# Second MLP product as seven half-size products per 512 tokens, streamed over the feature blocks

## The chip, the cores and the metric

The kernel runs on one core of a Trainium2 chip. The metric is the device time of one execution in microseconds (us). Engines are named as the profile names them: PE is TensorE (matmul), PEld its weight load, DVE is VectorE, ACT is ScalarE, POOL is GpSimd, SP is SyncE, which only issues DMAs here. Each engine takes its instructions strictly in the order in which they stand in its queue.

## The reference

An attention over 8 batches, 8 heads, 576 tokens and head size 64 feeds an MLP with 4608 tokens, width 512 and 2048 features:

```python
scores = scale * np.matmul(q, k.transpose(0, 1, 3, 2))
thresh = np.max(scores, axis=-1, keepdims=True) - tau
scores = np.where(scores >= thresh, scores, -1000000000.0)
attn = softmax(scores)                 # exp, sum, 1e-9 in the denominator
x = matmul(attn, v)                    # heads side by side: 4608 x 512
h = x @ w_in                           # first product, 512 x 2048
g = h * np.tanh(softplus(h))           # the gate, called Mish
return (g @ w_out).astype(np.float32)  # second product, 2048 x 512
```

The inputs q, k and v are float32; w_in and w_out are float64 and reach the chip as pairs of 32-bit words.

## The kernel before

Every large product is done with split operands: an operand is a rounded high part plus a low part with the rest, and of the four partial products three are made (high by high, high by low, low by high), accumulated in PSUM. Splitting costs a cast to the high part (on ACT, here and there on DVE) and a subtraction for the low part (on DVE or POOL).

The program has three stretches. For most of the span attention tiles run, and between them the first product of an earlier batch is fed in small portions by a generator (`gemm1`, `advance`). Its result h goes from PSUM to the staging tile `hst` (four feature blocks of 128 x 288) and by DMA to DRAM tiles `hd`, one for each 288 tokens. The last batch's first product is 384 matmuls, issued as 32 units of 12 (the loop over `u`, L780); in that loop the preparation of the second product is placed by tables of unit numbers (`PACE`, `H0`, `GATES`, `H1`, `GATES1`). Then comes the second product (L839 to L855).

Preparing w_out means decoding float64: ACT scales both words (`first`, L134 and L135), DVE clamps, shifts and joins the sign (L138, L141, L148), POOL adds the low word (L151), ACT casts the high part (L154), and DVE or POOL subtracts for the low part (L157). Before, this is done in 32 portions of 128 x 256, ordered by output block `d`: the first output block's weights are decoded in the last batch's loop, the rest during the first part of the second product. Preparing h means a DMA from `hd` (`load_h`), Mish on ACT (L679), a cast (L681 on DVE or L683 on ACT) and a subtraction on DVE (L684).

The second product goes over chunks of tokens, 256, then eight of 512, then 256. For each chunk and each of four output blocks one PSUM bank takes 3 x 16 matmuls; DVE copies it out (L854) and SP stores it. That is 1920 matmuls, 1536 with 512 columns and 384 with 256.

The lines behind which everything stands are few:

```python
for a, b in ((wh, gh), (wh, gl), (wlo, gh)):
    nc.tensor.matmul(o[:, :m], a, b, start=n == 0, stop=n == 3 * NF - 1)
```

SBUF is handed over between the stretches. The pool `wr` lies where the attention's tiles were; `er` opens in the 18th unit, where the first half of the first product's weights was; `wl` opens after the last unit, where `hst`, the split x and the other half of those weights were, so that a tile in it can be written only after the first product's last matmul and its last stores.

Of the kernel before, what the change touches and what calls it, by code (L numbers as in the profile page):

```python
# [5 lines left out]
F32 = mybir.dt.float32  # L6
# [31 lines left out]
NC = 512  # L38
PACE = {(0, 1, 2, 3, 5, 6, 8, 9, 16, 18, 20, 22, 27, 28)[i]: i for i in range(NF // 2 + 6)}
H0 = (2, 4, 11, 18)  # L40
GATES = (10, 17, 21, 24)
H1 = (8, 9, 22, 23)
GATES1 = (13, 15, 19, 20, 27, 29)
GATES2 = (1, 3)
CHUNKS = (0, *range(256, B * S, NC), B * S)
# [114 lines left out]
def attention_moe(tc, q, k, v, tau, w_in, w_out, out):  # L160
# [3 lines left out]
    with ExitStack() as outer:  # L164
# [3 lines left out]
        hd = [dram.tile([P, NF, HB], F32, name=f"hd{i}") for i in range(NBLK)]  # L168
# [6 lines left out]
        with ExitStack() as first:  # L175
# [6 lines left out]
            with ExitStack() as att:  # L182
# [262 lines left out]
                def gemm1(b, xs, pool=psh, tag="ph", first=1):  # L445
# [12 lines left out]
                    def parts(c, f, ds):  # L458
                        if (c, f) not in banks:
                            banks[c, f] = pool.tile([P, 512], F32, name="h", tag=tag)  # L460
# [198 lines left out]
            pso = second.enter_context(tc.tile_pool(name="pso", bufs=6, space=PSUM))  # L659

            def slot(pool, shape, kind, tag="g"):

                return pool.tile(shape, kind, name="g", tag=tag, bufs=2 if tag == "g" else 1)

            def small(kind, shape):
                return wr.tile(shape, kind, name="ht", tag="ht", bufs=2)

            def load_h(ht, c, fs):

                at, end = CHUNKS[c], CHUNKS[c + 1]  # L670
                while at < end:
                    i, off = divmod(at, HB)
                    m = min(HB - off, end - at)
                    to = at - CHUNKS[c]
                    nc.sync.dma_start(ht[:, :, to:to + m], hd[i][:, fs, off:off + m])
                    at += m

            def gate(ht, gh, gl, engine, vector=False):
                nc.scalar.activation(ht, ht, AF.Mish)  # L679
                if vector:  # L680
                    nc.vector.tensor_copy(gh, ht)  # L681
                else:
                    nc.scalar.copy(gh, ht)  # L683
                engine.tensor_tensor(gl, ht, fv(gh), ALU.subtract)  # L684

            def quarter(k):
                return slice(4 * k, 4 * k + 4)

            def weights2(pool, d):
                return [pool.tile([P, NF, P], F32R, name=f"w2{n}{d}") for n in "hl"]  # L690

            n0 = CHUNKS[1]
            w2 = [weights2(wr, 0)]
            homes = []
            for tag in "ab":
                four = slot(wr, [P, 4, 4 * WC], U32, tag)
                homes += [four[:, i] for i in range(4)]
            g0 = [slot(wr, [P, NF, n0], F32R) for _ in "hl"]
            work = {}
            h0 = {}  # L700
            h1 = {}
            g1 = []
            QUARTER = NF // 2

            def fetch(i):

                if i >= ND * QUARTER:
                    return
                if i < QUARTER:
                    st = homes[i]  # L710
                elif (i - QUARTER) % 6 < 4:
                    st = homes[4 + (i - QUARTER) % 6]
                else:
                    st = small(U32, [P, 4 * WC])
                work[i] = Decode(nc, st, None, None)
                d, k = divmod(i, QUARTER)
                for e in range(2):
                    f = 2 * k + e
                    src = w_out[f * P:(f + 1) * P, d * P:(d + 1) * P].bitcast(U32).rearrange("p (n t) -> p n t", t=2)
                    nc.sync.dma_start(work[i].words[:, e * P:(e + 1) * P], src)  # L720

            def middle(i):
                work[i].clamp()
                work[i].shift()
                work[i].sign()
                work[i].add()

            def finish(i, upper, lower):
                d, k = divmod(i, QUARTER)
                hi, lo = (w[:, 2 * k:2 * k + 2].rearrange("p f n -> p (f n)") for w in w2[d])  # L730
                work[i].hi, work[i].lo = hi, lo
                if upper is nc.scalar:
# [6 lines left out]
                elif i >= QUARTER:  # L739
                    fetch(i + 6)  # L740
# [161 lines left out]
```

## Time and profile before

| | |
|---|---|
| runs shown, median (lowest to highest) | 1371.6 us (1370.14 to 1371.99) |
| span of the profiled execution, which is its own time | 1370.5 us |
| PE busy | 1352.6 us (99%) |
| PEld / DVE / ACT / POOL busy | 1225.3 / 1001.6 / 943.0 / 771.8 us |
| first and last matmul of the second product start at | 968.41 and 1366.95 us |
| last batch's first product, 384 matmuls of 288 columns | about 917.4 to 968.4 us |

PE's busy time is summed from matmul records that overlap, since matmuls are pipelined: a 512-column matmul has a record of 392 ns, while about 220 of them start in 50 us. What a matmul costs is therefore read as the distance between starts. In the grouped rows a group's idle time and its releaser say what the engine waited for just before.

### The profile page before, as it was taken

How to read it: one execution, taken by the hardware profiler on the slowest of the kernel's cores; microseconds unless marked ns; L12 is line 12 of the kernel's file. 1: busy time of each engine (PE TensorE's matmuls, PEld its weight loads, DVE VectorE, ACT ScalarE, POOL GpSimd, SP SyncE). 2: the span in 40 equal slices, each digit the busy share in tenths (PEclk: the TensorE clock that was granted, in tenths of full speed). 3: DMA queues.
4: the chain of work that ended last, by engine and by line, in shares of the span. 5: the costliest groups of instructions: out<-in, count | busy, mean ns of one | idle time of the engine just before them, and what ended most of it. 6: DMA issues, size and time to landing. Idle time of an engine off the chain costs nothing.

```text
span 1370.5 us, 27694 instructions
## 1 busy us (share of the span) xinstructions
PE 1352.6 (99%) x8839; PEld 1225.3 (89%) x8839; DVE 1001.6 (73%) x2976; ACT 943.0 (69%) x2106; POOL 771.8 (56%) x1115
## 2 busy tenths in 40 slices
PE   9998899999999999999999999999999999999999
PEld 7555889999999999999999999999887888888888
DVE  6999999999999999999999999957874332232210
ACT  5878788888888888888888888856555543443210
POOL 5778888778788787887887878633460000000000
PEclk9999999999999999999999999999999999999999
DMA  5333323333333233332332323128655553543310
GB/s 152 98 98 107 114 80 114 108 96 103 101 99 115 89 120 93 111 107 97 103 112 88 124 90 110 60 88 277 196 164 151 153 148 102 143 131 102 93 52 23
DMA packets 126017, 154.64 MB, mean 113 GB/s; under 512 B 23472, under 2 KB 109488, under 8 KB 125872
## 3 DMA queue, kind: packets, MB, share of 16 engines
q1 hardware_dynamic: 124720, 148.16, 36.1%
q10 hardware_dynamic: 1152, 4.72, 0.9%
q8 instruction: 70, 1.15, 0.4%
q14 instruction: 75, 0.61, 0.1%
HBM read 105.64 MB, written 47.19 MB: 112 GB/s over the span
## 4 chain that ended last, share of the span: by engine, by line
PE 84%; DVE 5%; ACT 4%; DMA 2%; issue 2%; POOL 2%; SPq 1%; ACTq 0%; DVEq 0%; POOLq 0%
PE h L94 25%; PE o L851 23%; PE s L94 13%; PE y L94 12%; PE tp L94 9%; PE t L94 1%; DVE st L94 1%; DVE g L94 1%; DVE p L94 1%; DVE dec L94 1%; POOL w2l L157 1%; DMA ht<-hd 1%; DMA g<-hd 1%; ACT e L94 1%; DMA g<-w_out 1%
## 5 line engine op out<-in xcount | busy, mean ns | idle before, releaser
L851 PE MATMUL o<-g,w2h 128*128 128x512 f32 (+1 forms) x1280 | 363.9, 370 | 0.8 <-DVE g L684 0.8
L94 PE MATMUL h<-xh,w1h 128*128 128x288 f32 x1024 | 302.8, 296 | 1.1 <-ACT hst L94 0.6
L94 PE MATMUL h<-xh,w1l 128*128 128x288 f32 x1024 | 302.6, 296 | 0.0
L94 PE MATMUL h<-xl,w1h 128*128 128x288 f32 x1024 | 302.6, 295 | 0.0
L94 POOL TENSOR_SCALAR p<-p,st 128x576 f32<-128x576 f32 x288 | 243.8, 846 | 58.2 <-DVE st L94 33.8
L851 PEld LDWEIGHTS o<-g,w2h 128*128 128x128 f32 x1280 | 231.7, 188 | 43.7 <-DVE g L684 1.1
L94 PE MATMUL s<-k,q 128*128 128x288 f32 (+1 forms) x1280 | 255.2, 324 | 8.2 <-DVE p L94 7.9
L94 DVE SCALAR_TENSOR_TENSOR p<-s,st,e 128x576 f32<-128x576 f32 x288 | 235.1, 816 | 20.5 <-ACT e L94 11.0
L94 ACT ACTIVATE e<-s,st 128x576 f32<-128x576 f32 x288 | 214.2, 744 | 36.0 <-DVE st L94 30.4
L851 PE MATMUL o<-g,w2l 128*128 128x512 f32 (+1 forms) x640 | 236.2, 369 | 0.0
L94 DVE TENSOR_REDUCE st<-s 128x1 f32<-128x576 f32 x288 | 216.7, 752 | 2.6 <-PE s L94 2.5
L94 PEld LDWEIGHTS s<-k,q 128*128 128x128 f32 (+1 forms) x1280 | 182.7, 190 | 38.1 <-DVE p L94 23.6
L94 DVE TENSOR_TENSOR lo<-tp,hi 128x512 fp32r<-128x512 f32 (+1 forms) x280 | 174.7, 632 | 49.2 <-ACT hi L94 42.5
L94 PEld LDWEIGHTS h<-xh,w1h 128*128 128x128 f32 x1024 | 193.1, 189 | 1.9 <-ACT hst L94 1.1
L94 PEld LDWEIGHTS h<-xh,w1l 128*128 128x128 f32 x1024 | 193.0, 188 | 0.0
L94 PEld LDWEIGHTS h<-xl,w1h 128*128 128x128 f32 x1024 | 192.9, 188 | 0.0
L94 PE MATMUL tp<-ident,p 128*128 128x128 f32 x1152 | 174.4, 274 | 3.3 <-DVE lo L94 2.1
L94 ACT CAST hi<-tp 128x512 fp32r<-128x512 f32 (+1 forms) x280 | 149.7, 545 | 36.1 <-PE tp L94 33.1
L684 DVE TENSOR_TENSOR g<-ht,g 128x1024 fp32r<-128x1024 f32 (+1 forms) x60 | 68.6, 1153 | 137.0 <-ACT g L683 137.0
L94 PEld LDWEIGHTS tp<-ident,p 128*128 128x128 f32 x1152 | 138.9, 140 | 13.4 <-issue 5.4
L679 ACT ACTIVATE ht<-ht 128x1024 f32<-128x1024 f32 (+1 forms) x60 | 60.2, 1003 | 115.5 <-DMA ht<-hd 111.0
L851 PEld LDWEIGHTS o<-g,w2l 128*128 128x128 f32 x640 | 120.3, 188 | 21.3
(87 smaller groups left out, 2223.0 us busy)
## 6 DMA issues: line engine op xcount, KB each, us to landing
hd<-hst SPq DMA_DIRECT2D x56, 576.0 KB, 3.4
r<-q SPq DMA_DIRECT2D x120, 160.0 KB, 2.3
r<-k SPq DMA_DIRECT2D x120, 160.0 KB, 2.3
ht<-hd SPq DMA_DIRECT2D x52, 288.0 KB, 3.2
r<-v SPq DMA_DIRECT2D x56, 160.0 KB, 2.3
dec<-w_in SPq DMA_DIRECT2D x32, 256.0 KB, 2.8
out_t<-ost SPq DMA_DIRECT2D x32, 256.0 KB, 2.9
g<-w_out SPq DMA_DIRECT2D x48, 128.0 KB, 3.0
```

The source lines that it names most:

```text
L94: made = method(*args, **kwargs)
L157: engine.tensor_tensor(self.lo, fv(self.a), fv(self.hi), ALU.subtract)
L679: nc.scalar.activation(ht, ht, AF.Mish)
L684: engine.tensor_tensor(gl, ht, fv(gh), ALU.subtract)
L851: nc.tensor.matmul(o[:, :m], a, b, start=n == 0, stop=n == 3 * NF - 1)
```

## The change

The second product is cut into halves along tokens (256 + 256), features (8 blocks + 8 blocks) and outputs (256 + 256), and Strassen's scheme in its variant with shared sums forms the four quarter results from seven products of sums in place of eight. For each pair of feature blocks (`j` and `j + 8`) and each 512 tokens one step `n` of the loop takes seven products x two output blocks x three split terms = 42 matmuls of 256 columns. There are 72 steps (9 chunks of tokens times 8 feature pairs). Fourteen accumulators of 128 x 256 fill seven PSUM banks over eight steps; then `leave` adds them into the four quarters on DVE (the first on ACT) and stores them.

The operands are sums. For each weight pair `j`, `split_w` makes four sums of 128 x 256 on DVE, ACT casts all seven operands at once (128 x 1792), and DVE (odd `j`) or POOL (even `j`) subtracts. For each step `n`, `combine` does Mish on 128 x 1024, one subtraction 128 x 512 on DVE and two 128 x 256 on POOL; `split_z` casts 128 x 1792 on ACT and subtracts 128 x 1792 on DVE. The split operands of a step have three homes, one each in `wr`, `er` and `wl`. A scratch of six tiles of 8 KB a partition holds both raw weights and raw h; a load waits for one of them to come free. The DRAM tiles become `[128, 8, 2, 256]`, one for each 256 tokens, so that a step reads 2 KB runs, and a store of 288 tokens is cut into two pieces. In the last batch all `hst` copies are on ACT. The decode is in portions of 128 x 512, and its places are in the table `steps` (units) and `late` (steps).

```diff
-NC = 512
...
-CHUNKS = (0, *range(256, B * S, NC), B * S)
+NJ = NF // 2
+QT = 256
+NG = B * S // (2 * QT) * NJ
+PRODUCTS = ((0, 1), (4, 5), (5, 3), (3, 4), (6, 0), (2, 6), (1, 2))
...
-        hd = [dram.tile([P, NF, HB], F32, name=f"hd{i}") for i in range(NBLK)]
+        hd = [dram.tile([P, NJ, 2, QT], F32, name=f"hd{i}") for i in range(B * S // QT)]
...
+                def store(queue, hst, at, f):
+                    half, j = divmod(f, NJ)
+                    off, end = 0, HB
+                    while off < end:
+                        i, to = divmod(at + off, QT)
+                        m = min(QT - to, end - off)
+                        queue.dma_start(hd[i][:, j:j + 4, half, to:to + m], hst[:, :, off:off + m])
+                        off += m
...
-                        if b < B - 1 or f % 2:
-                            nc.scalar.copy(hst[:, f % 4], h[:, :HB])
-                        else:
-                            nc.vector.tensor_copy(hst[:, f % 4], h[:, :HB])
+                        nc.scalar.copy(hst[:, f % 4], h[:, :HB])
                         if f % 4 == 3:
-                            queue = nc.sync if b < B - 1 else nc.scalar
-                            queue.dma_start(hd[2 * b + c][:, f - 3:f + 1, :], hst)
+                            store(nc.sync if b < B - 1 else nc.scalar, hst, (2 * b + c) * HB, f - 3)
...
+            def bank(name):
+                i = taken[0] % 8
+                taken[0] += 1
+                if i < 6:
+                    return pso.tile([P, 512], F32, name=name, tag=f"o{i}")
+                return shared(name)
+            def scratch(name):
+                return wr.tile([P, 2048], F32, name=name, tag="z", bufs=6)
...
+            def load_w(j):
                 for e in range(2):
+                    y = scratch("w").bitcast(U32)
+                    words = y[:, 1024:].rearrange("p (n t) -> p n t", t=2)
+                    f = j + e * NJ
+                    nc.sync.dma_start(
+                        words, w_out[f * P:(f + 1) * P].bitcast(U32).rearrange("p (n t) -> p n t", t=2)
+                    )
+                    parts[j, e] = (y, words, y[:, 512:1024], y[:, :512])
+            def convert(j):
+                for e in (1, 0):
+                    _, words, a, _ = parts[j, e]
+                    top, low = words[:, :, 1], words[:, :, 0]
+                    nc.scalar.activation(fv(a), fv(top), AF.Copy, scale=2.0**-112)
+                    nc.scalar.activation(low, low, AF.Copy, scale=2.0**-29)
+            def compose(j):
+                for e in (1, 0):
+                    _, _, a, b = parts[j, e]
+                    nc.vector.tensor_scalar(fv(b), fv(a), TOP_MAX, -TOP_MAX, ALU.min, ALU.max)
+                    nc.vector.tensor_scalar(a, b, 3, 0x7FFFFFF8, ALU.logical_shift_left, ALU.bitwise_and)
+                    nc.vector.scalar_tensor_tensor(b, b, 0x80000000, a, ALU.bitwise_and, ALU.bitwise_or)
+                y, wy, ay, by = parts[j, 1]
+                _, wx, ax, bx = parts[j, 0]
+                nc.gpsimd.tensor_tensor(ay, by, wy[:, :, 0], ALU.add)
+                nc.gpsimd.tensor_tensor(ax[:, QT:], bx[:, QT:], wx[:, QT:, 0], ALU.add)
+                nc.gpsimd.tensor_tensor(y[:, QT:2 * QT], bx[:, :QT], wx[:, :QT, 0], ALU.add)
+            def split_w(j, engine):
+                y, a21 = fv(parts.pop((j, 1))[0]), fv(parts.pop((j, 0))[2])[:, QT:]
+                y = y.rearrange("p (n t) -> p n t", t=QT)
+                nc.vector.tensor_tensor(y[:, 4], a21, y[:, 3], ALU.add)
+                nc.vector.tensor_tensor(y[:, 6], a21, y[:, 1], ALU.subtract)
+                nc.vector.tensor_tensor(y[:, 5], y[:, 4], y[:, 1], ALU.subtract)
+                nc.vector.tensor_tensor(y[:, 7], y[:, 2], y[:, 5], ALU.subtract)
+                home = homes["wr" if j < 4 else "er" if j < 5 else "wl"]
+                w2[j] = [home.tile([P, 7, QT], F32R, name=f"w2{n}{j}") for n in "hl"]
+                nc.scalar.copy(w2[j][0], y[:, 1:])
+                engine.tensor_tensor(w2[j][1], y[:, 1:], fv(w2[j][0]), ALU.subtract)
+            def load_z(n):
+                if n < NG:
+                    c, j = divmod(n, NJ)
+                    z[n] = scratch("z").rearrange("p (n t) -> p n t", t=QT)
+                    for at, i in ((0, 2 * c + 1), (2, 2 * c)):
+                        nc.sync.dma_start(z[n][:, at:at + 2], hd[i][:, j])
+            def combine(n):
+                if n < NG:
+                    y = z[n]
+                    nc.scalar.activation(y[:, :4], y[:, :4], AF.Mish)
+                    nc.vector.tensor_tensor(y[:, 4:6], y[:, :1].to_broadcast([P, 2, QT]), y[:, 1:3], ALU.subtract)
+                    nc.gpsimd.tensor_tensor(y[:, 6], y[:, 1], y[:, 5], ALU.subtract)
+                    nc.gpsimd.tensor_tensor(y[:, 7], y[:, 6], y[:, 3], ALU.subtract)
+            def split_z(n):
+                if n < NG:
+                    home = homes[("wr", "er", "wl")[n % 3]]
+                    g[n] = [home.tile([P, 7, QT], F32R, name=f"g{m}", tag=f"g{m}") for m in "hl"]
+                    y = z.pop(n)
+                    nc.scalar.copy(g[n][0], y[:, 1:])
+                    nc.vector.tensor_tensor(g[n][1], y[:, 1:], fv(g[n][0]), ALU.subtract)
+            homes["wr"] = wr
+            steps = {}
+            for j in range(5):
+                steps.setdefault(max(0, 4 * j - 8), []).append(lambda j=j: load_w(j))
+                steps.setdefault(4 * j + 1, []).append(lambda j=j: convert(j))
+                steps.setdefault(4 * j + 3, []).append(lambda j=j: compose(j))
+            for j in range(5):
+                steps.setdefault(4 * j + 6, []).append(lambda j=j: split_w(j, nc.vector if j % 2 else nc.gpsimd))
+            steps.setdefault(13, []).append(lambda: load_w(5))
+            steps.setdefault(17, []).append(lambda: load_w(6))
+            for n in range(2):
+                steps.setdefault(20 + n, []).append(lambda n=n: load_z(n))
+            steps.setdefault(24, []).append(lambda: convert(5))
+            steps.setdefault(25, []).append(lambda: compose(5))
+            steps.setdefault(26, []).append(lambda: combine(0))
+            steps.setdefault(27, []).append(lambda: split_z(0))
+            steps.setdefault(28, []).append(lambda: combine(1))
+            steps.setdefault(29, []).append(lambda: convert(6))
+            steps.setdefault(29, []).append(lambda: split_z(1))
+            steps.setdefault(30, []).append(lambda: compose(6))
...
-            stream = gemm1(B - 1, batches[B - 1], pso, "o", 4)
+            stream = gemm1(B - 1, batches[B - 1], bank, 4)
...
+        late = {
+            0: [lambda: split_w(5, nc.vector), lambda: load_w(7), lambda: load_z(2), lambda: load_z(3), lambda: combine(2)],
+            1: [lambda: split_w(6, nc.gpsimd), lambda: load_z(4)],
+            2: [lambda: convert(7)],
+            3: [lambda: compose(7)],
+            4: [lambda: split_w(7, nc.vector)],
+        }
...
+            if k == 0:
+                sums["c"] = held()
+                nc.scalar.copy(sums["c"], o)
+            elif k == 1:
+                sums["u"] = held()
+                add(sums["u"], o, sums["c"])
+            elif k == 2:
+                sums["v"] = held()
+                add(sums["v"], o, sums["u"])
+            elif k == 3:
+                value = held()
+                add(value, o, sums["v"])
+                put(value, 1, 1)
+                add(sums["u"], o, sums["u"])
+            elif k == 4:
+                add(sums["u"], o, sums["u"])
+                put(sums["u"], 0, 1)
+            elif k == 5:
+                add(sums["v"], sums["v"], o, ALU.subtract)
+                put(sums["v"], 1, 0)
+            else:
+                add(sums["c"], o, sums["c"])
+                put(sums["c"], 0, 0)
+
+        for n in range(NG):
+            c, j = divmod(n, NJ)
+            for step in late.get(n, ()):
+                step()
+            if n > 0:
+                load_z(n + 4)
+            combine(n + 3)
+            split_z(n + 2)
+            if j == 0:
+                banks = [bank("o").rearrange("p (n t) -> p n t", t=QT) for _ in PRODUCTS]
+            for k, (wi, gi) in enumerate(PRODUCTS):
+                for b in range(2):
+                    at = slice(b * P, (b + 1) * P)
+                    for i, (x, y) in enumerate(((0, 0), (0, 1), (1, 0))):
+                        nc.tensor.matmul(
+                            banks[k][:, b], w2[j][x][:, wi, at], g[n][y][:, gi],
+                            start=j == b == i == 0, stop=j == NJ - 1 and b == 1 and i == 2,
+                        )
+                if j == NJ - 1:
+                    leave(k, c, banks[k])
+            g.pop(n)
```

Three places in the engines' queues matter. The first is ACT in the last batch's loop, where weights are decoded between the copies of h out of PSUM (`hst<-h`) and their stores. Before:

```order
L94 ACTIVATE g<-g 128x256 x2
L94 CAST w2h_15356<-g 128x256
L94 COPY hst<-h 128x288
L94 DMA hd_77<-hst 128x1152
L94 ACTIVATE g<-g 128x256 x2
L94 CAST w2h_15356<-g 128x256
L94 COPY hst<-h 128x288
```

Now (`w` is the scratch of a weight pair, `w2h` its cast):

```order
L90 ACTIVATE w<-w 128x512 x4
L90 COPY hst<-h 128x288
L90 CAST w2h_15623<-w 128x1792
L90 COPY hst<-h 128x288 x2
L90 DMA hd_79<-hst 128x4x32
L90 DMA hd_80<-hst 128x4x256
L90 COPY hst<-h 128x288
```

A pair's whole cast, which needs all the sums of that pair, now stands in one piece ahead of the next copies of h, and each store is two issues.

The second is POOL in the same loop, with the tiles' numbers. Before, three of the rows are low parts of weights (`w2l`), each of 128 x 256, and the others are additions of low words:

```order
L94 TENSOR_TENSOR w2l0_15357<-g_15358,w2h0_15356 128x256
L94 TENSOR_TENSOR g_15358<-g_15358 128x256
L94 TENSOR_TENSOR w2l0_15357<-g_15358,w2h0_15356 128x256
L94 TENSOR_TENSOR g_15359<-g_15359 128x256 x2
L94 TENSOR_TENSOR w2l0_15357<-g_15359,w2h0_15356 128x256
```

Now the first three rows add the low words of pair 0, the fourth is pair 0's low part, and the next three belong to pair 1:

```order
L90 TENSOR_TENSOR w_15416<-w_15416 128x512
L90 TENSOR_TENSOR w_15414<-w_15414 128x256
L90 TENSOR_TENSOR w_15416<-w_15414 128x256
L90 TENSOR_TENSOR w2l0_15540<-w_15416,w2h0_15539 128x1792
L90 TENSOR_TENSOR w_15420<-w_15420 128x512
L90 TENSOR_TENSOR w_15418<-w_15418 128x256
L90 TENSOR_TENSOR w_15420<-w_15418 128x256
```

Pair 1's additions stand behind pair 0's low part, which waits for ACT's cast of pair 0.

The third is ACT where the first product ends and the second begins; `gh_16014` belongs to step 1, `gh_16102` to step 2, `z_16088` and `z_16091` are the raw h of steps 2 and 3, and `hst_16008` is the last staging tile:

```order
L90 CAST gh_16014<-z_15856 128x1792
L90 COPY hst_16008<-h_16018 128x288
L90 COPY hst_16008<-h_16041 128x288
L90 COPY hst_16008<-h_16055 128x288
L90 DMA hd16_79<-hst_16008 128x4x32
L90 DMA hd17_80<-hst_16008 128x4x256
L90 CAST w2h5_16080<-w_15687 128x1792
L90 ACTIVATE z_16088<-z_16088 128x1024
L90 ACTIVATE z_16091<-z_16091 128x1024
L90 CAST gh_16102<-z_16088 128x1792
```

The cast for step 2 stands behind the cast of weight pair 5, which is written into `wl`, and behind the Mish of step 3. Before, the same stretch of this queue held portions of 128 x 256 of the second output block's weights and the Mish and casts of the second chunk.

More of the change, by code (lines that the diff above doesn't have):

```diff
@@ L443, in split_x, with shared, gemm1 @@
                     return parts
-                def gemm1(b, xs, pool=psh, tag="ph", first=1):
+                def shared(name):
+                    return psh.tile([P, 512], F32, name=name, tag="ph")
+                def store(queue, hst, at, f):
[6 more added lines that the diff above has]
+                        off += m
+                def gemm1(b, xs, bank=shared, first=1):
                     halves = (range(NF // 2), range(NF // 2, NF))
@@ L459, in parts @@
                         if (c, f) not in banks:
-                            banks[c, f] = pool.tile([P, 512], F32, name="h", tag=tag)
+                            banks[c, f] = bank("h")
                         h = banks[c, f]
@@ L678, in gate @@
[L678 to L690, printed above, removed]
@@ L774, in attention_moe @@
-            for i in range(QUARTER):
-                fetch(i)
+            pso = second.enter_context(tc.tile_pool(name="pso", bufs=1, space=PSUM))
+            taken = [0]
+            def bank(name):
[6 more added lines that the diff above has]
+                return wr.tile([P, 2048], F32, name=name, tag="z", bufs=6)
@@ L821, in attention_moe @@
-        for i in range(QUARTER, ND * QUARTER):
-            if QUARTER + 6 <= i + 2 < ND * QUARTER:
-                work[i + 2].first()
-            if QUARTER + 6 <= i + 1 < ND * QUARTER:
-                middle(i + 1)
-            if i - QUARTER in GATES2:
-                gate_h1(6 + GATES2.index(i - QUARTER))
-            finish(i, nc.scalar, nc.gpsimd)
-        h2 = slot(wr, [P, 8, NC], F32, "a")
-        for k in range(2):
-            load_h(h2[:, quarter(k)], 2, quarter(k))
-        ready = {0: [[g[:, quarter(q)] for g in g0] for q in range(4)], 1: [(pair[:, 0], pair[:, 1]) for pair in g1]}
@@ L834, in attention_moe @@
-        last = len(CHUNKS) - 2
-        steps = [(c, (d,), range(0)) for d in range(ND) for c in range(2)]
-        steps[-3] = (*steps[-3][:2], range(1))
-        steps[-1] = (*steps[-1][:2], range(1, 4))
-        steps += [(c, range(ND), range(4)) for c in range(2, last + 1)]
-        for c, ds, qs in steps:
-            if c < last:
-                ready.setdefault(c + 1, []).extend(make_g(c + 1, q, h2 if c == 1 and q < 2 else None) for q in qs)
-            m = CHUNKS[c + 1] - CHUNKS[c]
-            g = ready[c]
-            for d in ds:
-                o = pso.tile([P, NC], F32, name="o")
-                n = 0
-                for f in range(NF):
-                    wh, wlo = (w[:, f] for w in w2[d])
-                    gh, gl = (x[:, f % 4] for x in g[f // 4])
-                    for a, b in ((wh, gh), (wh, gl), (wlo, gh)):
-                        nc.tensor.matmul(o[:, :m], a, b, start=n == 0, stop=n == 3 * NF - 1)
-                        n += 1
-                ost = wl.tile([P, NC], F32, name="ost", bufs=2)
-                nc.vector.tensor_copy(ost[:, :m], o[:, :m])
-                nc.sync.dma_start(out[d * P:(d + 1) * P, CHUNKS[c]:CHUNKS[c + 1]], ost[:, :m])
+        wl = homes["wl"] = second.enter_context(tc.tile_pool(name="wl", bufs=1, side="left"))
@@ new lines, in attention_moe, with held @@
+        late = {
[5 more added lines that the diff above has]
+        }
+        places = out.rearrange("(n p) t -> p n t", p=P)
+        def held():
+            return wl.tile([P, 2, QT], F32, name="c", tag="c", bufs=6)
+        sums = {}
@@ new lines, in leave, with put, add @@
+        def leave(k, c, o):
+            def put(value, n, half):
+                at = (2 * c + half) * QT
+                nc.sync.dma_start(places[:, 2 * n:2 * n + 2, at:at + QT], value)
+            def add(to, a, b, op=ALU.add):
+                nc.vector.tensor_tensor(to, a, b, op)
+            if k == 0:
[21 more added lines that the diff above has]
+                put(sums["c"], 0, 0)
```

130 lines of the change are left out of this document (9 added, 121 removed).

## The prediction

> **What bounds the kernel now.** I read the page first, then the chain of waits and the busy times by stage.
>
> ```profile
> span 1370.5 us, 27694 instructions
> PE 1352.6 (99%) x8839; PEld 1225.3 (89%) x8839; DVE 1001.6 (73%) x2976; ACT 943.0 (69%) x2106; POOL 771.8 (56%) x1115
> ...
> 1046.07 321.17 PE o L851 x1493
> ```
>
> PE sets the time, and the chain's last piece is the second product alone, for 321 us without a break. What it costs is read from the stages and from starts in the timeline (start, us, instruction).
>
> ```profile
> 917.40:968.40 51.00, 49.94 (x370) 49.08 (x369) 33.72 (x67) 30.90 (x64) 14.33 (x18) 1.00 0.86 268
> 968.40:1367.10 398.70, 397.94 (x1922) 333.66 (x1920) 138.94 (x173) 152.18 (x196) 35.88 (x44) 1.00 0.41 118
> 1200.00:1250.00 50.00, 50.00 (x220) 41.03 (x219) 13.47 (x14) 18.23 (x18) 0.00 (x0) 1.00 0.39 111
> ...
> 968.41 0.40 PE L851 MATMUL o<-g,w2h 128*128 128x256 f32 x2
> 1344.48 0.40 PE L851 MATMUL o<-g,w2h 128*128 128x256 f32 x2
> 1366.95 0.28 PE L851 MATMUL o<-g,w2l 128*128 128x256 f32 x1
> ```
>
> A 512-column matmul takes 50/220 = 0.227 us of the line. The last chunk's 192 matmuls of 256 columns take 1366.95 - 1344.48 = 22.5 us for 191 intervals, 0.117 us each: half the columns cost slightly more than half, though each loads its own weights. The second product runs from 968.41 to 1367.23 us, 398.8 us; 1536 x 0.227 + 384 x 0.117 = 394 of that is work, so hardly anything is waited for at the seam. In the 51 us ahead of it (first row: PE, PEld, DVE, ACT, POOL busy) DVE, ACT and POOL have room.
>
> **The gain.** The new product is 72 x 42 = 3024 matmuls of 256 columns: 3024 x 0.117 = 353.8 us, 45.0 less than 398.8. Columns fall by an eighth, and part of that goes back because all matmuls are now short. Stretches of this row's kind vary from 0.115 to 0.120, which makes 348 to 363.
>
> **What preparation costs.** Prices for the new sizes come from these rows.
>
> ```profile
> L679 ACT ACTIVATE ht<-ht 128x1024 f32<-128x1024 f32 x52 | 55.1, 1060 | 103.9 <-DMA ht<-hd 99.4 <-DVE ost L854 4.4
> L683 ACT CAST g<-ht 128x1024 fp32r<-128x1024 f32 x52 | 54.0, 1049 | 35.3 <-PE o L851 34.1
> L683 ACT CAST g<-ht 128x512 fp32r<-128x512 f32 x8 | 4.9, 620 | 12.4 <-PE o L851 12.2
> L684 DVE TENSOR_TENSOR g<-ht,g 128x1024 fp32r<-128x1024 f32 x52 | 63.2, 1224 | 124.1 <-ACT g L683 124.1
> L684 DVE TENSOR_TENSOR g<-ht,g 128x512 fp32r<-128x512 f32 x8 | 5.5, 692 | 12.9 <-ACT g L683 12.9
> L94 DVE TENSOR_SCALAR ht<-ht 128x256 uint32<-128x256 uint32 x2 | 0.6, 294 | 0.1
> 945.60 0.69 DVE L94 CAST g<-g 128x1024 fp32r<-128x1024 f32 x1 [1.67 <-DMA ht<-hd]
> L94 POOL TENSOR_TENSOR ht<-ht 128x256 uint32<-128x256 uint32 x2 | 1.5, 744 | 7.8 <-ACT g L135 6.7 <-DVE ht L94 1.1
> L94 POOL TENSOR_TENSOR k<-r,k 128x320 fp32r<-128x320 f32 x120 | 104.6, 877 | 9.9 <-ACT k L94 6.7
> ```
>
> ACT: 0.62 us for 512 elements and, by the slope (1049 - 620)/512, 1.7 for 1792. DVE with two inputs: 0.43 for 256, 0.69 for 512, 2.0 for 1792; with one input 0.43 for 512, between 0.29 for 256 and 0.69 for 1024. POOL: 0.75 for 256, and by (877 - 744)/64 ns an element 1.3 for 512 and 3.8 for 1792.
>
> When DVE and POOL work at once, both slow down:
>
> ```profile
> 978.44 1.85 DVE L681 CAST g<-g 128x1024 fp32r<-128x1024 f32 x2 [1.77 <-DMA hd<-hst]
> 978.77 5.49 POOL L157 TENSOR_TENSOR w2l<-g,w2h 128x256 fp32r<-128x256 f32 x4 [1.23 <-ACT w2h L94]
> 980.21 3.44 DVE L684 TENSOR_TENSOR g<-g 128x1024 fp32r<-128x1024 f32 x2
> ```
>
> Four POOL subtractions take 5.5 us instead of 3.0, two DVE subtractions beside them 3.4 instead of 2.45. Together they get through 0.7 + 0.55 = 1.25 engines' work, not 2.
>
> **One weight pair.** The queues put pair j+1's additions on POOL behind pair j's low part. From the end of DVE's sums of an even pair: ACT cast 1.7, POOL low part 3.8, POOL additions of the next pair 1.3 + 0.75 + 0.75, DVE's four sums 1.4 (the first under the last addition): 9.7. From an odd pair: cast 1.7, DVE low part 2.0, DVE decode of the next pair 2 x (0.43 + 0.43 + 0.69) = 3.1, POOL's last two additions 1.5, sums 1.4: 9.7. Overlap of DVE with POOL adds by the rows above some 0.3 to the first and 1.0 to the second: 20.7 us for two pairs. The table allows four units of 12 x 0.133 = 1.6 us, 6.4 a pair. So the units don't set this pace; the chain does.
>
> ```profile
> 917.60 1.57 POOL L94 TENSOR_TENSOR xl<-x,xh 128x288 fp32r<-128x288 f32 x2 [0.55 <-ACT xh L94]
> 919.20 8.47 SPq L720 DMA_DIRECT2D g<-w_out  x16
> 922.23 0.77 ACT L94 ACTIVATE g<-g 128x256 f32<-128x256 f32 x2 [4.37 <-DMA g<-w_out]
> L94 ACT ACT_TABLE_LOAD x1 | 1.3, 1283 | 0.0
> L94 ACT COPY hst<-h 128x288 f32<-128x288 f32 x240 | 93.9, 400 | 36.8 <-PE h L94 35.7
> hd<-hst ACTq DMA_DIRECT2D x7, 576.0 KB, 4.9
> out_t<-ost SPq DMA_DIRECT2D x32, 256.0 KB, 2.9
> ```
>
> The loads start at 919.2, when POOL leaves the attention's tiles, in both kernels. The first 128 KB were there after 3.0 us. Pair 0 is 1 MB, at the stage's 268 GB/s 3.9 us: about 924. Conversion 0.6, decode 3.1 + 0.4, two additions 1.5 and sums 1.4 give 931 for pair 0's sums, and 931 + 2 x 20.7 = 972.4 for pair 4's.
>
> **Step 0, +19.9 us.** Its raw h needs the scratch tile that pair 4's sums release. Load 3.5 (2.9 plus the second issue): 975.9. ACT meanwhile casts pair 4, converts pair 5, copies h and loads the table: 979.4. Mish 1.06, DVE 0.69 (0.5 late behind pair 5's decode), two POOL subtractions behind pair 5's additions: 984.4; cast 1.7, low part 2.0: 988.3 against 968.41. The first product ends late too, at some 977, because its copies out of PSUM wait on ACT behind the casts; that is hidden under the same wait. Step 1 is ready in time.
>
> **Step 2, +14.0.** Its tile is in `wl`. On ACT the last copies of h stand behind step 1's cast (992.3), so the last store is issued at 994.1 and lands 4.9 later, at 999. Then come the cast of pair 5 (DVE's sums for it end at 1000.7), 1002.5; DVE's low part, 1004.6, which frees the tile for step 3's raw h; that load, 1008.1; step 3's Mish, which stands ahead of step 2's cast, 1009.2; cast 1010.8, low part 1013.3 with overlap. PE finishes step 1 at 999.4.
>
> **Steps 3, 5 and 6, +10.4.** Each step needs 2.75 of ACT and 2.7 of DVE in 4.9, which fits, but pairs 6 and 7 still have 4 to 9 us of casts, decodes, sums and low parts ahead in the queues. Step 3 waits 4.1, step 5 2.0, step 6 4.3.
>
> **The rest, +5.0.** At the end of each chunk DVE has seven more operations from PSUM, 7 x 0.69 = 4.8. Over eight steps that is 8 x 2.7 + 4.8 = 26.4 of 39.3 us, so it hides under PE, with 3.0 at the edges and 0.9 for a bank in step 0. Without this cover (every overlap stretched) DVE's 26.4 and POOL's 8 x 1.5 would fill 38.4 of 39.3. After the last matmul two additions of 0.7 and a store of 2.9 to 3.0 follow, 4.4 instead of 3.3: +1.1. The 16 copies of h that move from DVE to ACT, 0.4 each, are in ACT's 979.4. The doubled stores of h on SP and the smaller runs cost nothing in the long stretch: they wait for the same copies, and two `hst` tiles cover them. If the cover went, ACT would stand there too.
>
> Sum: 1370.5 - 45.0 + 19.9 + 14.0 + 10.4 + 5.0 = 1374.8 us of span. The median shown is 1.1 above the profiled span: **1376 us**.
>
> The TensorE clock is 1.00 in every stage quoted, and no PE wait here is long enough to test it. The Trainium skill, TensorE: Matmul & The Clock Gate, HAM oscillation, says that an idle gap over about 3.4 us drops PE to half clock until it has been busy as long. Three of my gaps are longer; two are followed by another wait that takes the loss up, so by this page the sum would be about 2 us more.
>
> **Rivals.**
>
> Slow overlap is absent. With the bare row prices the pair chain is 18.9 for two, step 0 starts at 983.6 (+15.2), step 2 costs 12.0, the later steps 7.2, the rest 2.9: 1362.8, or 1364 against the runs. For it stands the mean of POOL's additions in the last batch's loop, hardly above 744 ns:
>
> ```profile
> L94 POOL TENSOR_TENSOR g<-g 128x256 uint32<-128x256 uint32 x12 | 9.5, 795 | 34.8 <-DVE g L94 27.0 <-ACT g L94 4.9 <-DMA g<-w_out 1.8
> ```
>
> Against: there POOL is idle most of the time, and the two rows above are from where it is not. Chance 0.22.
>
> The units do set the pace. If the chain kept 6.4 us a pair, all would be ready at 968.4 and only the end and chunk edges remain: 1370.5 - 45.0 + 5.0 = 1330.5, 1332 against the runs. For it: POOL is busy only 14.3 us in the 51 before. Against: it needs 9.7 us of dependent rows to fit 6.4. Chance 0.08.
>
> DVE and POOL exclude each other. If one waits wholly for the other, two pairs take 22.5, step 0 starts at 994.3 (+25.9), step 2 waits 15.3, steps 3 to 7 16, and DVE's 26.4 plus POOL's 12 leave about 1 us per chunk, so the edges cost 13 and the end 1.1: 1397, 1398 against the runs. It decides from where overlap costs more than the whole shorter operation. For it: the four POOL rows. Against: there the four of POOL, the two subtractions and the two casts of DVE, 3.0 + 2.45 + 1.4 = 6.85 us one after the other, were done in 5.8. Chance 0.20. The Trainium skill, SBUF — State Buffer, Who interferes with whom, speaks for it: the port pair that DVE (with two SBUF inputs) and GpSimd share is an exclusive lock, and the later one fully blocks. The rows show it in part.
>
> **How the numbers follow.** The forecast has 0.50, with its own range 1366 to 1386 (0.115 to 0.120 a matmul is -6 to +9, the start of the loads ±2). A run can be told from no change at 0.2%, 2.7 us. Faster: 0.08, most of the 0.22 and a little of the forecast, 0.30. Slower: 0.20 and 0.30 of the forecast, 0.50. Same: 0.20. The range reaches to the two overlap rivals' ends, 1360 to 1398, and leaves out the units' rival and the outer edges.
>
> **What would show it.** Right: PE starts at 0.117 in steady stretches; first L-o matmul near 988 with `gl` on DVE named as releaser; a second wait of some 14 us after two steps; casts of `w2h` waiting for DVE and POOL about 10 us apart. Wrong: a first step before 975, a pair in under 8 us, a pitch of 0.13 or more (0.01 is 30 us), or waits at every chunk.

## The result and the profile after

The changed kernel takes 1386.3 us (1386.04 to 1386.82) against 1371.8 (1370.14 to 1373.15) of the kernel before, run beside it: 1.0106 times as long, 95% interval 1.0092 to 1.0121. It is slower by 1.1%. Its profiled execution spans 1384.1 us, 13.6 more than the one before.

The page of the changed kernel: its span, the busy times, and the strips of PE and of the granted clock, in which a dip stands where the first product meets the second. The last two rows are the costliest groups of the second product, with the idle time ahead of them.

```profile
span 1384.1 us, 30033 instructions
PE 1320.4 (95%) x9943; PEld 1254.4 (91%) x9943; DVE 1139.4 (82%) x3027; ACT 999.3 (72%) x2075; POOL 915.7 (66%) x1227
...
PE   9998899999999999999999999998657999999998
...
PEclk9999999999999999999999999999889999999999
...
L90 PE MATMUL o<-gh,w2h 128*128 128x256 f32 x1008 | 285.8, 284 | 23.3 <-ACT gh L90 21.5
...
L90 PE MATMUL o<-gl,w2h 128*128 128x256 f32 x1008 | 285.7, 283 | 9.6 <-DVE gl L90 9.6
```

The chain of waits ends, as before, with one unbroken piece of PE (start, us):

```profile
1065.74 309.41 PE o L90 x2634
```

That is 0.1175 us a matmul. From 1065.74 on PE is always fed, so the arithmetic that was saved was saved in time too. Nearly everything lost lies before; only the end, from the last matmul to the end of the span, takes 5.4 us instead of 3.3. The busy times by stage of the changed kernel (window, its length, then PE, PEld, DVE, ACT, POOL, granted clock, DMA share, GB/s):

```profile
917.40:968.40 51.00, 44.18 (x310) 43.48 (x310) 36.68 (x45) 25.24 (x46) 20.32 (x16) 0.93 0.58 189
968.40:1000.00 31.60, 18.04 (x113) 17.12 (x113) 17.92 (x23) 15.94 (x24) 13.16 (x12) 0.78 0.42 128
1000.00:1040.00 40.00, 22.16 (x156) 21.05 (x156) 27.88 (x27) 17.12 (x15) 21.34 (x15) 0.83 0.34 105
1080.00:1200.00 120.00, 120.00 (x1024) 120.00 (x1024) 80.83 (x70) 67.02 (x53) 50.63 (x50) 1.00 0.43 135
```

In the timeline of the changed kernel the second product starts at 989.44 and waits for over 1 us at steps 0, 2, 3, 5 and 6 (start, us, instruction, in brackets the idle time before it and who ended it; the rows between are left out):

```profile
989.44 0.58 PE L90 MATMUL o<-gh,w2h 128*128 128x256 f32 x1 [7.90 <-ACT gh L90]
991.50 0.58 PE L90 MATMUL o<-gl,w2h 128*128 128x256 f32 x1 [1.48 <-DVE gl L90]
1014.58 0.58 PE L90 MATMUL o<-gh,w2h 128*128 128x256 f32 x1 [11.36 <-ACT gh L90]
1016.64 0.58 PE L90 MATMUL o<-gl,w2h 128*128 128x256 f32 x1 [1.48 <-DVE gl L90]
1027.03 0.38 PE L90 MATMUL o<-gl,w2h 128*128 128x256 f32 x1 [2.94 <-DVE gl L90]
1039.68 0.39 PE L90 MATMUL o<-gl,w2h 128*128 128x256 f32 x1 [1.82 <-DVE gl L90]
1047.10 0.38 PE L90 MATMUL o<-gh,w2h 128*128 128x256 f32 x1 [2.25 <-ACT gh L90]
1049.16 0.58 PE L90 MATMUL o<-gl,w2h 128*128 128x256 f32 x1 [1.68 <-DVE gl L90]
```

A step has one matmul that needs only the cast (`gh`); then it waits for the low part (`gl`), which comes 2 us later. The start is set by the weight pairs. These rows of the same timeline are ACT's cast of pairs 0, 1 and 4 (two rows left out between), each right behind the pair's sums:

```profile
931.11 1.71 ACT L90 CAST w2h<-w 128x1792 fp32r<-128x1792 f32 x1 [0.32 <-DVE w L90]
942.03 1.69 ACT L90 CAST w2h<-w 128x1792 fp32r<-128x1792 f32 x1 [4.59 <-DVE w L90]
...
974.54 1.69 ACT L90 CAST w2h<-w 128x1792 fp32r<-128x1792 f32 x1 [6.78 <-DVE w L90]
```

Four pairs in 43.4 us, 10.9 each. Why it takes so long shows between the first two, in POOL's low part of pair 0 and DVE's decode of pair 1:

```profile
932.89 4.10 POOL L90 TENSOR_TENSOR w2l<-w,w2h 128x1792 fp32r<-128x1792 f32 x1 [3.29 <-ACT w2h L90]
932.92 4.35 DVE L90 TENSOR_SCALAR w<-w 128x512 uint32<-128x512 uint32 x1
936.94 1.50 POOL L90 TENSOR_TENSOR w<-w 128x512 uint32<-128x512 uint32 x1
937.31 1.69 DVE L90 SCALAR_TENSOR_TENSOR w<-w 128x512 uint32<-128x512 uint32 x1
```

DVE's shift, 0.43 us by itself, has a record of 4.35 us. It ends 0.3 us after POOL's 4.10. The next one, 0.69 by itself, takes 1.69 beside POOL's 1.50. A blocked instruction counts as busy here: DVE's busy time contains its waiting.

### The profile page after: what moved, and what is told of

Read it like the earlier page. It is cut to its first block, busy times and chain, and to the rows that moved or that the text cites. A ratio compares the mean times of both kernels' runs of the same rounds, so it can differ in the third digit from the quotient of the medians.

```text
span 1384.1 us, 30033 instructions
## 1 busy us (share of the span) xinstructions
PE 1320.4 (95%) x9943; PEld 1254.4 (91%) x9943; DVE 1139.4 (82%) x3027; ACT 999.3 (72%) x2075; POOL 915.7 (66%) x1227
## 5 line engine op out<-in xcount | busy, mean ns | idle before, releaser
L90 PE MATMUL o<-gh,w2h 128*128 128x256 f32 x1008 | 285.8, 284 | 23.3 <-ACT gh L90 21.5
L90 PE MATMUL o<-gl,w2h 128*128 128x256 f32 x1008 | 285.7, 283 | 9.6 <-DVE gl L90 9.6
L90 PE MATMUL o<-gh,w2l 128*128 128x256 f32 x1008 | 284.7, 282 | 0.0
L90 POOL TENSOR_TENSOR z<-z 128x256 f32<-128x256 f32 x144 | 148.4, 1036 | 200.1 <-DVE z L90 194.4
L90 DVE SCALAR_TENSOR_TENSOR p<-s,st,e 128x576 f32<-128x576 f32 x288 | 235.1, 816 | 21.3 <-ACT e L90 11.7
L90 DVE TENSOR_TENSOR gl<-z,gh 128x1792 fp32r<-128x1792 f32 x72 | 148.5, 2062 | 110.6 <-ACT gh L90 110.6
L90 ACT CAST gh<-z 128x1792 fp32r<-128x1792 f32 x72 | 121.9, 1693 | 151.4 <-POOL z L90 81.7
L90 PEld LDWEIGHTS o<-gh,w2h 128*128 128x128 f32 x1008 | 193.9, 192 | 24.4 <-ACT gh L90 22.1
L90 PEld LDWEIGHTS o<-gl,w2h 128*128 128x128 f32 x1008 | 193.8, 192 | 11.2 <-DVE gl L90 11.2
L90 PEld LDWEIGHTS o<-gh,w2l 128*128 128x128 f32 x1008 | 193.9, 192 | 0.0
```

The costliest lines, as they stand in the source:

```text
L90: made = method(*args, **kwargs)
```

## The experiments

Theory A: DVE and POOL hardly ever work at the same time on these operations, so the preparation at the seam is one amount of work for the two together, and an operation on POOL costs its own, longer time. Theory B: it is a chain of dependent instructions, which only has to be put in another order. Further rivals were that POOL's help pays (C), that the second product itself loses time, and that half clock after idle time does (H).

**Low parts later.** The low part of pairs 0 to 4 moves behind the next pair's decode.

```diff
-                engine.tensor_tensor(w2[j][1], y[:, 1:], fv(w2[j][0]), ALU.subtract)
+                lows[j] = lambda: engine.tensor_tensor(w2[j][1], y[:, 1:], fv(w2[j][0]), ALU.subtract)
...
+            for j in range(5):
+                steps.setdefault(4 * j + 8, []).append(lambda j=j: low_w(j))
```

> The low parts of weight pairs 0 to 4 are issued two units later, behind the next pair's decode instead of ahead of it; the engines stay the same and nothing is left out. In the changed kernel the sums of pairs 0 to 4 end 10.85 us apart, POOL's low part of 4.0 us stands in that chain, and the second product starts at 989.4. Theory A (DVE and POOL hardly work at the same time, so the preparation is a fixed amount of work of the two engines together): the order changes little, pairs stay about 10.4 us apart, start at 986 to 989, span 1380 to 1384. Theory B (a chain of dependent instructions, in which the low part merely stands in front): without the low part a pair takes about 7 us, the start moves to about 972, span about 1369.

Measured: 1382.5 us, 1.0078 [1.0063, 1.0093] of before; span 1381.3. The second product starts at 986.52, and the pairs' casts stand at 932.42, 943.34, 952.03, 962.92 and 971.59, 9.8 us apart on average. That is theory A's case, with pairs a little closer than its 10.4. The timeline of this kernel shows where the freed time went:

```profile
937.92 4.26 POOL L90 TENSOR_TENSOR w2l<-w,w2h 128x1792 fp32r<-128x1792 f32 x1
938.18 5.07 DVE L90 TENSOR_TENSOR w<-w 128x256 f32<-128x256 f32 x3
```

Three sums, 0.42 us each, now take 5.07: the low part no longer blocks the decode, it blocks the sums.

**Weight work on DVE.** Same order; the additions of the low words and all low parts go to DVE.

```diff
-                nc.gpsimd.tensor_tensor(ay, by, wy[:, :, 0], ALU.add)
+                nc.vector.tensor_tensor(ay, by, wy[:, :, 0], ALU.add)
...
-                steps.setdefault(4 * j + 6, []).append(lambda j=j: split_w(j, nc.vector if j % 2 else nc.gpsimd))
+                steps.setdefault(4 * j + 6, []).append(lambda j=j: split_w(j, nc.vector))
```

> All weight work of POOL (the additions of the low words and the low parts) goes to DVE; order and amount stay. DVE needs 2.0 us for a low part where POOL needs 4.0, and about 1.3 for the three additions where POOL needs 2.8 to 3.4. Theory A (the two engines exclude each other, so only the sum of both counts): the sum falls by 2.0 or 4.0 us a pair, minus what did overlap: pairs 10.0 us apart or less, start at 984 to 987, span 1378 to 1382. Theory C (the two really work side by side, POOL's help is worth its time): DVE becomes the longer queue, start at 990 or later, span 1385 or more.

Measured: 1375.7 us, 1.0026 [1.0015, 1.0037]; span 1374.1, start at 982.94, casts 9.6 us apart (931.84 to 970.11 for four). C falls: one engine is faster than the two. The gain of 10.0 us is more than A's 2 to 6, since pairs 6 and 7 and the steps behind the start gain too. The move takes away both the blocking and POOL's longer times; no run separates the two.

**Both edits.**

> Both edits: the low parts behind the next pair's decode, and all weight work on DVE. Theory A: DVE alone has 8.35 us a pair (decode 3.1, additions 1.3, sums 1.4, low part 2.0, gaps 0.5) and waits for ACT no more; start at about 979, span about 1373. Theory B (chain): no better than the later low parts alone, about 1369 if those give 1369. Theory C (POOL's help is worth its time): slower than the later low parts alone by 5 us or more.

Measured: 1367.2 us, 0.9966 [0.9953, 0.9979], below the kernel before; span 1365.4, start at 974.31, casts 7.5 us apart (931.51 to 961.42 for four). Better than A's numbers; the order pays once POOL is out of the way, 8.7 us against 2.8 with POOL. DVE's groups from 922 to 1045 us, first row the changed kernel, second this one (count, busy us, mean ns):

```profile
L90 DVE TENSOR_SCALAR w<-w 128x512 uint32<-128x512 uint32 x16 | 20.6, 1287 | 0.5
```

```profile
L90 DVE TENSOR_SCALAR w<-w 128x512 uint32<-128x512 uint32 x16 | 6.8, 427 | 0.5
```

The same 16 shifts in 6.8 us instead of 20.6. What little POOL still does here, the subtractions of h, is blocked in its turn. In this kernel's timeline DVE's low part of h and POOL's first subtraction:

```profile
1028.40 2.02 DVE L90 TENSOR_TENSOR gl<-z,gh 128x1792 fp32r<-128x1792 f32 x1
...
1028.56 2.45 POOL L90 TENSOR_TENSOR z<-z 128x256 f32<-128x256 f32 x1 [5.55 <-DVE z L90]
```

An operation of 0.74 us takes 2.45 and ends 0.6 after DVE's.

**Less decode.**

```diff
-                    nc.vector.tensor_scalar(a, b, 3, 0x7FFFFFF8, ALU.logical_shift_left, ALU.bitwise_and)
-                    nc.vector.scalar_tensor_tensor(b, b, 0x80000000, a, ALU.bitwise_and, ALU.bitwise_or)
...
-                nc.gpsimd.tensor_tensor(ay, by, wy[:, :, 0], ALU.add)
...
-                nc.vector.tensor_tensor(y[:, 4], a21, y[:, 3], ALU.add)
```

> Leaves work out, so the output is not the reference's: of each pair's decode the shift, the joining of the sign and the additions of the low words, and the four sums of weights; loads, conversion, clamp, casts, low parts and the whole second product stay. If the loss is in the preparation at the seam: pairs follow the units at 6.4 us or less, the second product starts at 968 to 975 with waits of under 10 us in all, span 1338 to 1355, and its pitch stays 0.117 to 0.118. If the second product itself has the loss (256-column matmuls, their weight loads, half clock): span above 1375 although the preparation is early.

Measured: span 1340.3 (one run, 1342.1 us). Casts 6.2 us apart at first, start at 964.3, earlier than expected, since the first product no longer waits for ACT; PE busy 120.00 of 120 us from 1080 to 1200. The second product itself is not at fault; without that work the seam gives back 43.8 us. Step 2 still waits here, 5.9 us for its cast.

**PE kept busy.** Extra matmuls fill PE's idle time ahead of steps 0 and 2.

```diff
+            if n == 0:
+                spare = bank("o").rearrange("p (n t) -> p n t", t=QT)
+            for to in {0: [banks[0][:, 0]] * 60, 2: [spare[:, 0]] * 108}.get(n, ()):
+                nc.tensor.matmul(to, w2[0][0][:, 0, :P], w2[0][0][:, 0], start=True, stop=True)
```

> The changed kernel with extra matmuls whose results nobody reads, so that PE does not fall idle: 60 of 256 columns ahead of step 0 (7.0 of the 7.9 us of idle) and 108 ahead of step 2 (12.6 of the 11.4 us of idle plus what steps 0 and 1 gain). Nothing is left out. The granted clock should then be 1.00 instead of 0.50 in the 5 us after each of the two starts. Theory H (half clock is a loss of its own): 2 to 2.5 us gained per start, span 1378 to 1380. Theory N (the wait behind takes it up: step 2 starts when its cast is done, about 1014.6, step 3 when its low part is there, about 1027.0, whatever PE did before): starts within 0.3 us of those, span 1383.5 to 1385.

Measured: 1388.2 us, 1.0123 [1.0110, 1.0137]; span 1386.2. The stretch behind step 2's start, the changed kernel first, then this one:

```profile
1014.50:1020.00 5.50, 3.94 (x16) 3.65 (x17) 3.99 (x5) 1.41 (x2) 2.61 (x1) 0.50 0.41 117
```

```profile
1014.50:1020.00 5.50, 4.96 (x41) 4.76 (x41) 3.99 (x5) 1.41 (x2) 3.35 (x2) 1.00 0.27 85
...
1027.79 0.58 PE L90 MATMUL o<-gl,w2h 128*128 128x256 f32 x1 [2.76 <-DVE gl L90]
```

The clock is 1.00 instead of 0.50 (behind step 0's start the cure was partial, 0.81), and still step 3 gets its low part no earlier, 1027.79 against 1027.03. H falls for step 2: what half clock takes there is taken from a wait. The other case of the expectation, N, by which the next wait takes the loss up, fits step 3, but the span is 1.2 above its range. The seam lies 0.5 us later already in the first product's last wait (977.06 against 976.57), and the bank that the extra matmuls use shifts the order of the banks. This run says nothing on the third dip, 0.79 from 1048.7 to 1056.7 us, which it leaves as it was.

**A new order, all on DVE.** The weight pairs and the first nine steps' h are cut into pieces (decode, additions, sums with cast, low part; load, Mish, subtractions, cast with low part), and a table places each. The order was worked out by adding up the queues with the durations of the kernel with both edits. Raw h of steps 0 and 3 is loaded ahead of most weights, the operands of steps 2 and 3 stand ahead of pair 5's low part, and step 4's ahead of pair 6's sums. In the table `lw`, `cv`, `c1`, `c2`, `su`, `lo` are a pair's load, conversion, decode, additions, sums with cast, and low part; `lz`, `mi`, `sz`, `gz` are a step's load, Mish, subtractions, and cast with low part.

```diff
+                    y, engine = z[n], nc.vector if n < 9 else nc.gpsimd
...
-                    nc.gpsimd.tensor_tensor(y[:, 6], y[:, 1], y[:, 5], ALU.subtract)
+                    engine.tensor_tensor(y[:, 6], y[:, 1], y[:, 5], ALU.subtract)
...
+            UNITS = (
+                "lw2 cv2 lz0",
...
+                "lw0 c12",
+                "cv0",
...
+                "lw1 mi0 c22",
+                "su2 lw3 cv1 c10 lz3",
...
+            LATE = (
+                "cv6 c25 su5",
+                "sz2 c16 mi4 sz4 c26 gz2",
+                "gz3 lo5 gz4 cv7 su6 c17 mi6 c27 mi5 sz5",
```

> All weight work on DVE as in the earlier run with both edits, the two small subtractions of the first nine steps' h on DVE too, and a new order of the same pieces: raw h of the first steps is fetched and prepared among the weight pairs, the operands of step 2 no longer stand behind pair 5, and each half of the decode and each low part has a place of its own. Nothing is left out. Theory A (DVE's and POOL's exclusive work plus the order at the seam is the whole loss): by the queues' durations in the trace of the run with both edits, step 0 starts when the first product ends, 968 to 970, step 2 at 981 to 984, step 8 at 1017 to 1020 (1040.1 there), so the span is 20 to 22 us shorter than 1365.4: 1343 to 1347, below the kernel before by 1.8 to 2%. If something else holds the steps back (DMA, clock, PSUM banks): step 2 still later than 990 and the span above 1355.

Measured: 1345.5 us, 0.9814 [0.9800, 0.9827], faster than both kernels; span 1344.7. PE's waits of over 1 us in the second product are one for a PSUM bank in step 0, those of step 2, and one of step 5:

```profile
973.16 0.39 PE L90 MATMUL o<-gh,w2h 128*128 128x256 f32 x1 [2.08 <-ACT hst L90]
...
983.17 0.58 PE L90 MATMUL o<-gh,w2h 128*128 128x256 f32 x1 [2.76 <-ACT gh L90]
986.99 0.58 PE L90 MATMUL o<-gl,w2h 128*128 128x256 f32 x1 [3.23 <-DVE gl L90]
...
1007.34 0.39 PE L90 MATMUL o<-gl,w2h 128*128 128x256 f32 x1 [2.44 <-DVE gl L90]
```

The first matmul starts at 967.3; step 2 comes 31.4 us earlier than in the changed kernel. Step 8 follows at 1023.0, some 3 us later than expected, within the span that was expected. From 1000 to 1020 DVE is the limit:

```profile
1000.00:1020.00 20.00, 17.26 (x141) 16.72 (x141) 18.99 (x23) 12.12 (x10) 0.00 (x0) 1.00 0.45 141
```

**The same order with POOL.** Additions, low parts of even pairs and h's two subtractions go back to POOL; two of the places, against the kernel with the new order:

```diff
-                nc.vector.tensor_tensor(ay, by, wy[:, :, 0], ALU.add)
+                nc.gpsimd.tensor_tensor(ay, by, wy[:, :, 0], ALU.add)
...
-                lows[j] = lambda: nc.vector.tensor_tensor(w2[j][1], y[:, 1:], fv(w2[j][0]), ALU.subtract)
+                lows[j] = lambda: (nc.vector if j % 2 else nc.gpsimd).tensor_tensor(w2[j][1], y[:, 1:], fv(w2[j][0]), ALU.subtract)
```

> The fastest kernel's order, with the work given back to the engines of the changed kernel: the three additions of each pair, the low parts of even pairs and the two small subtractions of h on POOL. Nothing is left out. Theory A (DVE and POOL exclude each other, so the amount counts): the kernel that only issued the low parts later needed 9.8 us a pair, and h takes 2.55 of DVE and 1.5 of POOL a step, so eight pairs and nine steps are 8 x 9.8 + 9 x 4.0 = 114 us after 924.6; step 8 starts at about 1039 instead of 1020, span 1360 to 1368. Theory O (the order alone made the gain): span within 4 us of 1344.7.

Measured: 1368.9 us, 0.9979 [0.9970, 0.9989]; span 1366.4, in A's range and 21.7 above the same order on DVE; but step 8 starts at 1045.05, 6 us later than A's 1039, since step 7 starts only at 1036.29; so A has the span and not the path. With the other runs this makes a table of spans:

| | weight work with POOL | on DVE |
|---|---|---|
| order of the changed kernel | 1384.1 | 1374.1 |
| new order | 1366.4 | 1344.7 |

The order alone brings 17.7 us, the engine alone 10.0, both 39.4, 11.7 more than the sum (the new order's DVE column includes h's two subtractions). So neither theory stands by itself: A sets how much work there is, and the order (B, in a wider form than low parts alone) how much of the time the engines have work at hand.

**No POOL in the second product at all.** Against the kernel with the new order:

```diff
-                    y, engine = z[n], nc.vector if n < 9 else nc.gpsimd
+                    y, engine = z[n], nc.vector
```

> The fastest kernel with the two small subtractions of h on DVE in all 72 steps, so that POOL is idle after the attention. Nothing is left out. It prices the exclusion where PE sets the pace: POOL's 128x256 subtraction takes 1.0 us there instead of 0.74. If PE covers it, the steady pitch stays 120.0 us of PE busy in 120 and the span within 1.5 us of 1344.7; if the chunk edges pay for it, 0.5 to 1.5 us a chunk, 4 to 12 us less.

Measured: span 1343.9; 1347.1 us (1345.42 to 1348.83), 0.9829 [0.9812, 0.9845], an interval that overlaps that of the kernel with POOL in later steps. PE is busy 120.00 of 120 us from 1080 to 1200 in both. Behind a PE that is always fed the exclusion costs nothing that these runs can tell.

## Why the prediction was right, and where its sum was not

The forecast of slower held, and for the reason given: the preparation at the seam costs more than the saved matmuls bring. But 1386.3 is 10 above the 1376, just past the upper end of the forecast's own range, and almost midway between it and the 1398 of the rival in which DVE and POOL exclude each other. The time alone does not decide between these two; the records do, and they speak for the rival's mechanism. Against the sum of 1374.8 the span is 9.3 longer.

**The gain, -45.0: right.** The pitch is 309.41/2634 = 0.1175 against 0.117; the difference is 1.3 us over the 2664 matmuls behind 1065.74. It was lost in rounding: the prediction's own 22.47 us over 191 intervals are 0.1176.

**The weight pairs: right in place, too small.** Pair 0's sums end at 931.0 as predicted, pair 4's at 974.5 instead of 972.4: 21.7 us for two pairs instead of 20.7. The step that failed is the one on overlap. It took the slowdown as partial, 1.25 engines' work, read from four POOL and two DVE subtractions of the kernel before; the records of the changed kernel show the later instruction blocked until the earlier one is nearly done. By the Trainium skill, SBUF — State Buffer, Who interferes with whom, the pair of ports that GpSimd shares with DVE's operations of two SBUF inputs, and with some of one input in a mode that uses both of DVE's ports, is held for a whole instruction and the other engine fully blocks; the 4.35 us of a one-input shift beside POOL's 4.10 agree.

The rows from which the 1.25 was read hold several operations each. One by one, in the timeline of the kernel before, four of them are:

```profile
980.21 1.76 DVE L684 TENSOR_TENSOR g<-g 128x1024 fp32r<-128x1024 f32 x1
980.85 1.72 POOL L157 TENSOR_TENSOR w2l<-g,w2h 128x256 fp32r<-128x256 f32 x1
981.89 1.76 DVE L684 TENSOR_TENSOR g<-g 128x1024 fp32r<-128x1024 f32 x1
982.53 1.72 POOL L157 TENSOR_TENSOR w2l<-g,w2h 128x256 fp32r<-128x256 f32 x1
```

They end in turn, at 981.97, 982.57, 983.65 and 984.25: DVE's second 1.08 us after POOL's first, POOL's 0.60 after DVE's, where alone they need 1.22 and 0.74. So the engines took turns there too, and what looked like a partial slowdown is some 0.14 us of overlap at each change of turn. Long operations change turn seldom: POOL's 4.10 and the shift's 0.43 took 4.38 together.

That the sum was off by only 1.0 for two pairs is in part luck: in this order the two engines wait for each other's results, or for ACT, much of the time anyway. Almost all of it lies in the low part on POOL and what it blocks, from an even pair to the next, 10.9 instead of 10.0. Of that, POOL's low part takes 4.1 where the prediction has 3.8; by the slope of its own two rows it should have had 3.9.

**Step 0, +19.9: 3.2 too small.** Its low part was to be there at 988.3 and came at 991.5. Of that 2.1 are the pairs. The releaser of the first matmul is the cast on ACT, not the low part as forecast, but nothing but one matmul can run before the low part.

**Step 2, +14.0: right.** Low part at 1016.6 instead of 1013.3; the 3.3 are, to 0.1, those of step 0. The path is the predicted one too: step 3's Mish waits for its load and stands ahead of step 2's cast.

```profile
1011.89 1.06 ACT L90 ACTIVATE z<-z 128x1024 f32<-128x1024 f32 x1 [3.96 <-DMA z<-hd]
1012.86 1.67 ACT L90 CAST gh<-z 128x1792 fp32r<-128x1792 f32 x1
```

**Steps 3, 5 and 6, +10.4: 2.6 too small.** By the working the three get their low parts at 1022.3, 1034.1 and 1043.3; they came at 1027.0, 1039.7 and 1049.2, 4.7, 5.6 and 5.9 later. The timeline of the changed kernel shows what stood ahead of step 3's:

```profile
1020.38 4.11 POOL L90 TENSOR_TENSOR w2l<-w,w2h 128x1792 fp32r<-128x1792 f32 x1 [3.21 <-ACT w2h L90]
...
1021.44 3.60 DVE L90 TENSOR_TENSOR z<-z 128x512 f32<-128x512 f32 x1 [2.86 <-ACT z L90]
...
1024.96 2.01 DVE L90 TENSOR_TENSOR gl<-z,gh 128x1792 fp32r<-128x1792 f32 x1
```

POOL's low part of pair 6 holds a DVE subtraction for a later step, 0.68 by itself, for 3.60, and step 3's low part stands behind that on DVE. Full blocking again, where the working had a partial slowdown.

**The rest, +5.0: 3.4 too small with the pitch.** From step 6's low part to the last matmul's end (1378.7) it is 329.5 instead of 327.1. Of these 2.4, 1.3 are the pitch; a dip of the clock to 0.79 over 8.0 us takes up to 1.7, and the first chunk's edge gives back 1.2 (1.3 and 0.5 instead of 3.0; later edges show no wait); some 0.6 is left unexplained. The end is 5.4 from the last matmul instead of 4.4. Together 3.2 + 0.1 + 2.6 + 2.4 + 1.0 = 9.3.

**The clock.** From the Trainium skill, TensorE: Matmul & The Clock Gate, HAM oscillation, the prediction had estimated about 2 us more. The clock does fall to 0.50 after waits of 8 and 11 us, as that section says of idle gaps over about 3.4 us. The prediction's reading that the next wait takes this up is borne out for step 2 by the run with extra matmuls. The dip behind step 6, with no long wait after it, was not tried.

**The rivals.** Units at 6.4 us a pair: only the kernel with less decode came there. No slowdown in overlap, 1364: excluded by the 4.35 (its 18.9 us for two pairs should also have been 19.4, twice the prediction's own 9.7). Full exclusion had the mechanism but not the time: of its 1398, 13 us were waits at the chunks' edges, of which 1.8 occur; in steady stretches DVE's 80.8 of 120 us leave room even though POOL's 128x256 takes 1.02 us there on average instead of 0.74. At the seam, too, it asked for more than was measured: 25.9 us for step 0 against 23.1, and 16 for the later steps against 13.0.

## What to carry to other kernels

Where the records show that two engines block each other, add their work up as if they were one engine, and give each piece to the one that does it in less time; a helper that needs twice as long takes that time from the one it helps. Check this by an operation's mean against its time alone, since a blocked instruction counts as busy, and look at operations one by one, since a row of several hides who waited. Not every two operations block each other. In the attention of the changed kernel these two start together and are both done within 0.89 us:

```profile
833.58 0.89 POOL L90 TENSOR_TENSOR k<-r,k 128x320 fp32r<-128x320 f32 x1
833.58 0.67 DVE L90 TENSOR_TENSOR lo<-tp,hi 128x512 fp32r<-128x512 f32 x1
```

One input of this DVE operation, `tp`, lies in PSUM; the blocked ones above have all their inputs in SBUF. Whether that is the reason was not tried.

A scheme that saves matmuls has to be paid for in preparation ahead of its first step: sum the work of the engines that prepare from the first load to the step where everything is there, and set the order so that no operand stands behind another that is needed later.

## What the runs showed that was not expected

A DVE shift of 0.43 us with a record of 4.35 beside a POOL subtraction. POOL's subtraction of 0.74 us with one of 2.45 beside DVE's of 2.02. And two edits worth 2.8 and 10.0 us alone that bring 18.7 together, because the first only moved the blocking to another instruction while POOL was still there.
